# Attention and feed-forward on one core: plain fp32 for the first batch and for the value products, and a new order of the last matmuls

## The chip, the cores and the metric

The kernel runs on one core of a Trainium2 chip. The metric is the device time of one execution in microseconds, the median of three runs. Engines: TensorE (PE), VectorE (DVE), ScalarE (ACT), GpSimd (POOL) and the queues that issue transfers, above all SP.

## The reference

For 8 batches of 8 heads, 576 tokens and 64 channels a head, the reference computes two attentions in a row. A pack of 32 queries p attends over the keys and values; then the tokens q attend over the packed result, which is both key and value. The result, laid out as 576 x 512, goes through a Fourier mixing and a feed-forward:

```python
p_packed = sm_attn(p, k, v)
x = sm_attn(q, p_packed, p_packed)           # then (B, S, 512)
mixed = real(fft(fft(x, axis=1), axis=2))
u = x + mixed
un = (u - mean(u)) / sqrt(var(u) + 1e-6)
out = u + maximum(un @ w_ch1, 0) @ w_ch2     # 512 -> 2048 -> 512
```

The inputs q, k and p are drawn with a spread of 0.8.

## The kernel before

**Precision.** Most matmuls are done as three: each operand is split into a high part (rounded to fp32r, which TensorE takes in one pass) and a low part (the rest), and the products high x high, high x low and low x high are summed in PSUM (`three`, L279). `split` (L106) makes the parts: ScalarE rounds, VectorE or GpSimd subtracts. Some small products are plain fp32.

**Attention of one batch** is `front(b)` (L284), in two groups g of four heads. Scores are exponentiated, turned, and multiplied with the values (`packed`, L415); the packed result pp is spread into a block-diagonal matrix bd (128 rows of 4 heads x 32, 256 columns) by GpSimd, and split into bdh and bdl (`diagonals`, L437). In the second attention the weights a are normalised (`weights`), folded over the token mirror into even and odd sums (`folded`, L547, tiles eo and f; `folded_rest`, L560, makes the remaining columns of f and the rounded xh, oh; `folded_parts`, L598, the low parts xl, ol, fl). The Fourier transform over channels acts on pp (`values_spectrum`, L505: turned products and a join, parts gh and gl). Products of f with the spectrum give y (`first_products`, L687, for batch 0; the loop at L741 for the others), `spectrum` (L627) transforms over tokens into pz, and `value` (L672) multiplies the folded weights with bd into px, six matmuls for 512 columns of output. `even` (L772) adds px and one spectrum to pe, `blocks` (L777) makes the rows of u and their sums. 32 remaining token pairs go the same way through `spectra_apart` (L637) and L812 to L820.

**Feed-forward** (`ffn`, L888) takes tiles of four blocks of 128 rows, nine tiles in all. For each of 16 chunks, `up` is 12 matmuls into ph, ScalarE and VectorE make hh and hl, and `down` adds 12 matmuls into four accumulators, one step behind. At the end (L973 to L976) VectorE adds each accumulator to u and SP sends it out. Weights are fetched in chunks by SP during the head and tile 0 and rebuilt by ScalarE (`top`, `lows`) and VectorE (`bits`).

**Order.** Within a manual schedule each engine works in program order. For batch 0 that order is the string `ORDER[0]` (L40): each letter calls a function with its digit, as `n0` for `diagonals` of group 0, `F` `folded_high`, `h` `folded_parts`, `J` and `H` the low parts of g and f, `j` the join, `P` `first_products`, `X` the first value products, `T` the tables, `i` idle matmuls (`i122`: 12, waiting for tile m). The other batches are spread over the feed-forward steps of the tile before; `y` marks a step. Idle matmuls (L727) write a bank that nobody reads.

The last feed-forward group, whole:

```python
down(NJ - 1, *prev, nxt.moves(late[1]) if nxt and len(late) > 1 else ())
for i in (2, 3, 0, 1):
    u = u_of[keys[i]]
    nc.vector.scalar_tensor_tensor(u, acc[i], stat_of[keys[i]][:, 2:3], u, ALU.mult, ALU.add)
    nc.sync.dma_start(out[(first + i) * P:(first + i + 1) * P, :], u)
```

Of the kernel before, what the change touches and what calls it, by code (L numbers as in the profile page):

```python
# [17 lines left out]
P = 128  # L18
# [21 lines left out]
ORDER = ("K0 K1 V0 I0 Q0 W0 V1 Q1 B0 W1 W2 W3 i70 s0 x0 s1 i40 t0 x1 w0 p0 b0 T0 t1 n0 d0 v0 z0 i20 W4 W5 W6 W7 W8 W9 q0 e0 p1 "  # L40
         "b1 T1 T2 i80 l0 d1 w1 w2 w3 w4 m0 q1 a0 e1 g0 i122 l1 f0 r0 w5 F0 m1 n1 g1 w6 w7 i203 a1 j0 w8 h0 J0 H0 P0 f1 r1 F1 i64 j1 h1 J1 X0 "
         "H1 v2 W10 P1",
# [24 lines left out]
FR, FA, FO = 256, 357, 421  # L67
# [16 lines left out]
def tile_kernel(ctx, tc, kpT, qT, v, w1, w2, tabH, tabL, tabR, tabF, tabB, tabT, sel, ident_d, out):  # L84
# [32 lines left out]
    nc.gpsimd.memset(bmask, 0.0)  # L117
    for h in range(4):
        nc.gpsimd.memset(bmask[h * NPK:(h + 1) * NPK, h:h + 1], 0.5)
    w1f = cpool.tile([P, NJ, DM], F32, name="w1f")  # L120
# [14 lines left out]

    def load_tables(i):
        todo = [(basis, tabB)] + [x for t in range(2) for x in ((tbh[t], tabH[t]), (tbl[t], tabL[t]), (tbr[t], tabR[t]))] + [(tbf, tabF)]
        for to, src in (todo[:1], todo[1:3], todo[3:])[i]:
            nc.gpsimd.dma_start(to, src)
# [144 lines left out]
    def front(b):  # L284
        kps, vts, qts, e1s, e1T, rinv, away = {}, {}, {}, {}, {}, {}, {}
        pp2s, ppT, pph, ppl, bdh, bdl = {}, {}, {}, {}, {}, {}
        s2s, zs, as_, fh, fl, xh, xl, oh, ol, gh, gl = {}, {}, {}, {}, {}, {}, {}, {}, {}, {}, {}
# [127 lines left out]
        def packed(g):  # L415
# [16 lines left out]
            def spread():  # L432
                bd = work.tile([P, 4, D], F32, tag="tmp", name="bd", bufs=3)
                nc.gpsimd.tensor_tensor(bd, pp2[:, 0:1, :].to_broadcast([P, 4, D]),
                                        bmask.unsqueeze(2).to_broadcast([P, 4, D]), ALU.mult)

                def diagonals():  # L437
                    bdh[g] = work.tile([P, 4 * D], F32R, tag="bdh", name="bdh")
                    bdl[g] = work.tile([P, 4 * D], F32R, tag="bdl", name="bdl")
                    split(bdh[g], bdl[g], bd.rearrange("p a d -> p (a d)"), nc.gpsimd)  # L440

                if b == 0:
                    late["n", g] = diagonals
                else:
                    after(1, diagonals)
# [59 lines left out]
        def values_spectrum(g):  # L505

            hi = work.tile([P, 2, N2], F32R, tag="gh", name="gh")
            lo = work.tile([P, 2, N2], F32R, tag="gl", name="gl")
# [16 lines left out]
            def join():  # L525
                for t in range(2):
                    TW[TA[min(b, 2)]].tensor_tensor(prod[0][:, t, :], prod[0][:, t, :], prod[1][:, t, :], ops[t])
                if b == 0:
                    nc.scalar.copy(hi, prod[0])
                    late["J", g] = lambda: nc.vector.tensor_tensor(lo, prod[0], hi.bitcast(F32), ALU.subtract)  # L530
                else:
                    after(1, lambda: split(hi, lo, prod[0], TW[TL[min(b, 2)]]))
# [14 lines left out]
        def folded(g):  # L547
# [3 lines left out]
            f = work.tile([P, FW], F32, tag="att", name="f", bufs=ATT)  # L551
# [6 lines left out]
            eos[g], fs[g] = eo, f  # L558

        def folded_rest(g):  # L560
# [14 lines left out]
            def edge(at, op):  # L575
# [11 lines left out]
            sm.tensor_scalar(f[:, FA:FA + 64].rearrange("p (i m k) -> p i m k", i=2, m=2), apart, 2.0, 1.0 / 16,  # L587
                             ALU.mult, ALU.add)
            xh[g] = work.tile([P, 256], F32R, tag="xh", name="xh")
            nc.scalar.activation(xh[g], ec[:, 0:256], AF.Copy, bias=1.0 / 16)  # L590
            oh[g] = work.tile([P, 256], F32R, tag="oh", name="oh")
            nc.scalar.copy(oh[g], oc[:, 0:256])

        def folded_high(g):
            fh[g] = work.tile([P, FW], F32R, tag="fh", name="fh")
            nc.scalar.copy(fh[g], fs[g])

        def folded_parts(g):  # L598

            eo, f = eos[g], fs[g]  # L600
            ec, oc = eo[:, 0, :], eo[:, 1, :]
            if g not in fh:
                folded_high(g)
            xl[g] = work.tile([P, 256], F32R, tag="xl", name="xl")
            nc.vector.scalar_tensor_tensor(xl[g], ec[:, 0:256], 1.0 / 16, xh[g].bitcast(F32), ALU.add, ALU.subtract)
            ol[g] = work.tile([P, 256], F32R, tag="ol", name="ol")
            (nc.vector, nc.gpsimd)[EO[min(b, 2)]].tensor_tensor(ol[g], oc[:, 0:256], oh[g].bitcast(F32), ALU.subtract)

            def low():
                fl[g] = work.tile([P, FW], F32R, tag="fl", name="fl")  # L610
                nc.vector.tensor_tensor(fl[g], f, fh[g].bitcast(F32), ALU.subtract)

            in_place("H", g, low)
# [8 lines left out]
                 "F": folded_high, "z": lambda _: next(splits)}  # L622
        for x in "xblnjJH":
            parts[x] = lambda g, x=x: late[x, g]()
        yh, yl, yr, ysum, ypx, spec = [], [], [], [], {}, {}

        def spectrum(t, q, tag=None):  # L627

            pz = bank("pz")
            w = slice(P * q, P * q + P)  # L630
            three(pz[:, :N2], tbh[t][:, w], tbl[t][:, w], yh[t][:, q, :], yl[t][:, q, :], True, False)
            nc.tensor.matmul(pz[:, :N2], tbr[t][:NRC[t], w], yr[t][:NRC[t]], start=False, stop=True)
            sb = (ffp if tag else work).tile([P, N2], F32, tag=tag or f"spec{t}", name=f"spec{t}", bufs=6 if tag else 1)
            nc.scalar.copy(sb, pz[:, :N2])
            return sb

        def spectra_apart(rows):  # L637
# [22 lines left out]
            else:  # L660
                remainders(True, False)
                strips([[yh[t].bitcast(F32), yl[t].bitcast(F32)] for t in range(2)], False, True)
# [9 lines left out]
        def value(ah, al, w, px=None):  # L672
            px = bank("px") if px is None else px
            for g in range(2):
                three(px[:, g * 256:(g + 1) * 256], ah[g][:, w], al[g][:, w], bdh[g], bdl[g], True, True)
            return px

        def window(sb, rows):
            w = sb[rows, 0:256]
            return bass.AP(tensor=w.tensor, offset=w.offset, ap=[list(w.ap[0]), [1, 2], [1, 256]])  # L680
# [3 lines left out]
        def halves(x):  # L684
            return x.rearrange("p (a c) -> p a c", a=2)

        def first_products(g):  # L687
# [4 lines left out]
            for t in range(2 * g):  # L692
                yh.append(work.tile([P, 2, N2], F32R, tag="att", name="yh", bufs=ATT))
                yl.append(work.tile([P, 2, N2], F32R, tag="att", name="yl", bufs=ATT))
# [5 lines left out]
            for t, c in outs:  # L700
                nr, w, py = place(t, c)
                nc.tensor.matmul(py[:nr, :N2], fh[g][:, w], gh[g][:, t, :], start=(g == 0), stop=False)
                nc.tensor.matmul(py[:nr, :N2], fh[g][:, w], gl[g][:, t, :], start=False, stop=False)
                if g == 0:
                    nc.tensor.matmul(py[:nr, :N2], fl[g][:, w], gh[g][:, t, :], start=False, stop=False)
            for t, c in outs if g else ():
                nr, w, py = place(t, c)
                nc.tensor.matmul(py[:nr, :N2], fl[g][:, w], gh[g][:, t, :], start=False, stop=True)
            for t, c in outs if g else ():
                nr, w, py = place(t, c)  # L710
                if c < 2:
                    split(yh[t][:, c, :], yl[t][:, c, :], py[:, :N2])
# [8 lines left out]
        def first_values():  # L721
            ypx["p", 0] = value(xh, xl, slice(1, 256, 2))
            ypx["q", 0] = value(oh, ol, slice(1, 256, 2), psf.tile([P, 512], F32, tag="ph", name="px"))
# [17 lines left out]
        for t, base in enumerate((0, FO) if b else ()):  # L741
# [23 lines left out]
            whole = work.tile([P, 2, N2], F32, tag=("ysum", "gh")[t], name="ysum", bufs=1 + t)  # L765
            for c in range(2):
                nc.scalar.copy(whole[:, c, :], pys[c][:, :N2])
            ysum.append(whole)
# [3 lines left out]
        def even(c, A, px):  # L772
            pe = work.tile([P, DM], F32, tag="tmp", name="pe", bufs=3)
            nc.vector.tensor_tensor(halves(pe), halves(px), window(A, allp), ALU.add)
            return pe

        def blocks(c, pe, Bs, px):  # L777
            qe = work.tile([P, DM], F32, tag="tmp", name="qe", bufs=3)
            nc.vector.tensor_tensor(qe[:, 0:256], px[:, 0:256], Bs[:, 0:256], ALU.subtract)
            nc.vector.tensor_tensor(qe[:, 256:512], px[:, 256:512], Bs[:, 1:257], ALU.add)  # L780
# [7 lines left out]
        def odd_values(c):  # L788
            return value(oh, ol, slice(1 - c, 256, 2))

        if b == 0:
            for t in range(2):
                spec[t, 1] = spectrum(t, 1, "wr")
            ypx["p", 1] = value(xh, xl, slice(0, 256, 2))
            ypx["q", 1] = odd_values(1)
# [16 lines left out]
        px = value(fh, fl, slice(FA - rows.start, FA - rows.start + P))  # L812
        xa = work.tile([P, DM], F32, tag="tmp", name="xa", bufs=3)
        nc.vector.tensor_tensor(halves(xa[rows]), halves(px[rows]), window(A, rows), ALU.add)
        ur = u_of[kr]
        nc.vector.tensor_tensor(ur[rows, 0:256], xa[rows, 0:256], Bs[rows, 0:256], ALU.subtract)
# [349 lines left out]
```

## Time and profile before

| | us |
|---|---|
| median of 3 runs (965.23 to 966.66) | 965.59 |
| profiled execution | 964.36 |
| its span | 962.2 |
| TensorE busy in the span | 944.4 |
| VectorE, ScalarE, GpSimd busy | 589.5, 452.3, 463.2 |

The span is the time between the first and the last instruction that the profiler saw on the core; the time of the execution has 2.16 us around it. A view by stretch gives the busy time of each engine and the clock granted to TensorE as a share of full speed. The chain of waits goes back from the last instruction to what released each step. A group of instructions by form has its count, its busy time and the mean of one in nanoseconds.

### The profile page before, as it was taken

How to read it: one execution, taken by the hardware profiler on the slowest of the kernel's cores; microseconds unless marked ns; L12 is line 12 of the kernel's file. 1: busy time of each engine (PE TensorE's matmuls, PEld its weight loads, DVE VectorE, ACT ScalarE, POOL GpSimd, SP SyncE). 2: the span in 40 equal slices, each digit the busy share in tenths (PEclk: the TensorE clock that was granted, in tenths of full speed). 3: DMA queues.
4: the chain of work that ended last, by engine and by line, in shares of the span. 5: the costliest groups of instructions: out<-in, count | busy, mean ns of one | idle time of the engine just before them, and what ended most of it. 6: DMA issues, size and time to landing. Idle time of an engine off the chain costs nothing.

```text
span 962.2 us, 15191 instructions
## 1 busy us (share of the span) xinstructions
PE 944.4 (98%) x5614; PEld 774.4 (80%) x5614; DVE 589.5 (61%) x1186; ACT 452.3 (47%) x930; POOL 463.2 (48%) x397
## 2 busy tenths in 40 slices
PE   7899999999999999999999999999999999999997
PEld 4777887788778887788778877888778888887886
DVE  5989967684667756794668466874679353123112
ACT  5689564444434444444444444454444443233331
POOL 3156534653555435643465355543555355445442
PEclk9999999999999999999999999999999999999999
DMA  9675125400340016200540045100600011001001
GB/s 358 220 268 190 42 84 164 136 1 1 128 152 37 1 44 209 85 1 25 165 148 0 1 140 166 55 1 23 212 30 23 16 50 44 22 23 45 1 0 44
DMA packets 48777, 80.74 MB, mean 84 GB/s; under 512 B 7088, under 2 KB 28464, under 8 KB 48704
## 3 DMA queue, kind: packets, MB, share of 16 engines
q1 hardware_dynamic: 42480, 69.62, 21.3%
q10 hardware_dynamic: 5184, 8.85, 2.9%
q0 software_dynamic: 1040, 1.31, 0.5%
q8 instruction: 44, 0.72, 0.3%
q14 instruction: 29, 0.24, 0.1%
HBM read 59.45 MB, written 20.32 MB: 83 GB/s over the span
## 4 chain that ended last, share of the span: by engine, by line
PE 93%; DVE 3%; ACT 2%; DMA 1%; issue 1%; ACTq 0%; DVEq 0%
PE acc L927 40%; PE ph L910 40%; PE po L424 1%; PE px L282 1%; PE px L280 1%; PE px L281 1%; PE s2T L329 1%; PE py L282 1%; PE py L280 1%; PE py L281 1%; PE s L329 1%; ACT e L356 1%; PE idle L730 1%; PE pz L653 0%; DMA kp<-kpT 0%
## 5 line engine op out<-in xcount | busy, mean ns | idle before, releaser
L110 POOL TENSOR_TENSOR wr_l<-w2f,wr_h 128x512 fp32r<-128x512 f32 x144 | 188.2, 1307 | 275.8 <-ACT wr_h L107 269.8
L110 POOL TENSOR_TENSOR wr_l<-w1f,wr_h 128x512 fp32r<-128x512 f32 x144 | 200.3, 1392 | 195.2 <-ACT wr_h L107 175.6
L917 DVE SCALAR_TENSOR_TENSOR hl<-ph,hh 128x512 fp32r<-128x512 f32 x144 | 98.7, 686 | 288.3 <-ACT hh L916 287.6
L910 PE MATMUL ph<-uh,wr_h 128*128 128x512 f32 (+1 forms) x580 | 226.1, 392 | 1.0 <-ACT uh L107 1.0
L927 PE MATMUL acc<-wr_h,hh 128*128 128x512 f32 x576 | 226.0, 392 | 0.0
L927 PE MATMUL acc<-wr_h,hl 128*128 128x512 f32 x576 | 224.8, 390 | 0.0
L927 PE MATMUL acc<-wr_l,hh 128*128 128x512 f32 x576 | 224.8, 390 | 0.0
L910 PE MATMUL ph<-ul,wr_h 128*128 128x512 f32 (+1 forms) x580 | 224.2, 388 | 0.5 <-DVE ul L110 0.5
L910 PE MATMUL ph<-uh,wr_l 128*128 128x512 f32 (+1 forms) x580 | 224.1, 388 | 0.0
L916 ACT ACTIVATE hh<-ph 128x512 fp32r<-128x512 f32 x144 | 86.2, 598 | 235.6 <-PE ph L910 221.7
L107 ACT CAST wr_h<-w1f 128x512 fp32r<-128x512 f32 x144 | 89.3, 620 | 185.2 <-POOL wr_l L110 79.3
L910 PEld LDWEIGHTS ph<-uh,wr_h 128*128 128x128 f32 x580 | 108.5, 188 | 29.3 <-DVE s L479 5.9
L927 PEld LDWEIGHTS acc<-wr_h,hl 128*128 128x128 f32 x576 | 108.1, 188 | 23.2
L910 PEld LDWEIGHTS ph<-uh,wr_l 128*128 128x128 f32 x580 | 108.5, 188 | 22.7
L910 PEld LDWEIGHTS ph<-ul,wr_h 128*128 128x128 f32 x580 | 108.6, 188 | 21.6 <-DVE ul L110 0.9
L927 PEld LDWEIGHTS acc<-wr_h,hh 128*128 128x128 f32 x576 | 108.2, 188 | 21.7
L927 PEld LDWEIGHTS acc<-wr_l,hh 128*128 128x128 f32 x576 | 108.2, 188 | 20.9
L107 ACT CAST wr_h<-w2f 128x512 fp32r<-128x512 f32 x144 | 88.3, 613 | 34.1 <-PE acc L927 26.8
L975 DVE SCALAR_TENSOR_TENSOR ubuf<-acc,stat,ubuf 128x512 f32<-128x512 f32 x36 | 24.6, 744 | 3.5 <-PE acc L927 3.5
L834 DVE TENSOR_SCALAR unp<-ubuf,stat 128x512 f32<-128x512 f32 x28 | 25.4, 907 | 1.0 <-POOL bdl L110 0.7
L254 ACT ACTIVATE junk<-ubuf,stat 128x512 f32<-128x512 f32 x36 | 25.8, 717 | 0.2 <-DVE stat L249 0.2
L110 DVE TENSOR_TENSOR yl<-py,yh 128x258 fp32r<-128x258 f32 x32 | 13.2, 425 | 18.5 <-ACT yh L107 17.8
(230 smaller groups left out, 1216.7 us busy)
## 6 DMA issues: line engine op xcount, KB each, us to landing
kp<-kpT SPq DMA_DIRECT2D x16, 608.0 KB, 4.3
out<-ubuf SPq DMA_DIRECT2D x36, 256.0 KB, 3.9
far<-unt SPq DMA_DIRECT2D x28, 256.0 KB, 2.0
back<-far SPq DMA_DIRECT2D x112, 64.0 KB, 2.0
qt<-qT ACTq DMA_DIRECT2D x12, 576.0 KB, 4.6
vt<-v SPq DMA_DIRECT2D x12, 512.0 KB, 3.8
w1f<-w SPq DMA_DIRECT2D x9, 512.0 KB, 6.6
w2f<-w SPq DMA_DIRECT2D x9, 512.0 KB, 6.4
```

The source lines that it names most:

```text
L107: copied = nc.scalar.copy(hi, src)
L110: (lo_eng or nc.vector).tensor_tensor(lo, src, hi.bitcast(F32), ALU.subtract)
L254: nc.scalar.activation(junk, u, AF.Square, bias=st[:, 1:2], scale=-sign, accum_out=st[:, 2:3])
L280: nc.tensor.matmul(o, lh, rh, start=first, stop=False)
L281: nc.tensor.matmul(o, lh, rl, start=False, stop=False)
L282: nc.tensor.matmul(o, ll, rh, start=False, stop=last)
L834: nc.vector.tensor_scalar(un, u_of[key].rearrange("p (c q d) -> p q c d", c=4, q=4), stat_of[key][:, 1:2], None, ALU.subtract)
L910: nc.tensor.matmul(ph[:, t], l[:, c * P:(c + 1) * P], r[:, c, t], start=(k == 0), stop=(k == 11))
L916: nc.scalar.activation(hh[:, :T], ph[:, :T], AF.Relu)
L917: nc.vector.scalar_tensor_tensor(hl[:, :T], ph[:, :T], 0.0, hh[:, :T].bitcast(F32), ALU.max, ALU.subtract)
L927: nc.tensor.matmul(acc[i], l[:, w], r, start=(j == 0 and k == 0), stop=(j == NJ - 1 and k == 2))
L975: nc.vector.scalar_tensor_tensor(u, acc[i], stat_of[keys[i]][:, 2:3], u, ALU.mult, ALU.add)
```

## The change

Batch 0 works in plain fp32 from the fold on: f, the joined spectrum and y have no high and low parts, the tables of `spectrum` are loaded whole (tabS), and the order of its steps is new. Its value products are fp32 with the 256-column bd. From batch 1 on the value products are plain fp32 too, with a bd of two heads (128 columns): the upper 64 rows (two heads) and the lower 64 rows are separate matmuls on their own half of the array, into a PSUM bank each. The last feed-forward group of the last tile is done in another order, its last block in two halves of columns. The core of the diff:

```diff
-... p0 b0 T0 t1 n0 d0 v0 z0 i20 W4 W5 W6 W7 W8 W9 q0 e0 p1 b1 T1 T2 i80 l0 d1 w1 w2 w3 w4 m0 q1 a0 e1 g0 i122 l1
-   f0 r0 w5 F0 m1 n1 g1 w6 w7 i203 a1 j0 w8 h0 J0 H0 P0 f1 r1 F1 i64 j1 h1 J1 X0 H1 v2 W10 P1
+... p0 b0 T0 t1 d0 v0 z0 i20 W4 W5 W6 W7 W8 W9 q0 e0 p1 b1 T1 i80 l0 d1 w1 w2 w3 w4 m0 q1 a0 e1 g0 i122 l1
+   f0 j0 r0 w5 m1 g1 P0 w6 w7 a1 f1 r1 j1 X0 w8 v2 W10 P1 T2
 def load_tables(i):
+    if i == 1:
+        whole.append(spot(0, 7, [P, 2, KT]))
+        todo = [(whole[0], tabS...)] + [(tbr[t], tabR[t]) for t in range(2)] + [(tbf, tabF)]
+    else:
+        todo = [(basis, tabB)] if i == 0 else [x for t in range(2) for x in ((tbh[t], tabH[t]), (tbl[t], tabL[t]))]
 def spread():
-    bd = work.tile([P, 4, D], F32, ...)
...
-    bdh[g], bdl[g] = ...; split(bdh[g], bdl[g], bd, nc.gpsimd)
+    mask, n = (bpair, 2) if b else (bmask, 4)
+    bd[g] = work.tile([P, n, D], F32, tag=f"bd{n}", name="bd")
 def join():
-    if b == 0:
-        nc.scalar.copy(hi, prod[0])
-        late["J", g] = lambda: nc.vector.tensor_tensor(lo, prod[0], hi, ALU.subtract)
+    # batch 0: the join writes gh itself, fp32
 def folded_rest(g):
-    f[:, FA:FA + 64] = ...
-    xh[g] = F32R; oh[g] = F32R
+    fa[g] = work.tile([P, D], F32, ...)
+    xs[g] = F32;  os_[g] = F32
 def folded_parts(g):
-    xl[g] = ...; ol[g] = ...
     fh[g], fl[g] = ...                       # batch 1 on only
 def spectrum(t, q, tag=None):
+    if b: three(...)
+    else: nc.tensor.matmul(pz[:, :N2], whole[0][:, t, w], yh[t][:, q, :], start=True, stop=False)
-def value(ah, al, w, px=None):
-    for g in range(2):
-        three(px[:, g * 256:(g + 1) * 256], ah[g][:, w], al[g][:, w], bdh[g], bdl[g], True, True)
+def values_of(*pairs, rows=slice(0, P), banks=(None, None)):
+    if b == 0:
+        # one fp32 matmul of 256 columns for each pair and g
...
+    banks = [bank("px") for _ in range(2)]
+    for k, (x, w) in enumerate(pairs):
+        for g in range(2):
+            for r in range(2):
+                at = slice(r * D, (r + 1) * D)
+                nc.tensor.matmul(banks[r][rows, k * 256 + g * P:k * 256 + (g + 1) * P], x[g][at, w], bd[g][at],
+                                 start=True, stop=True, tile_position=(r * D, rows.start))
+def add_even(to, px, A, rows):
+    for x, cols in pieces(px):
+        nc.vector.tensor_tensor(halves(to[rows])[:, :, cols], x[rows], window(A, rows, cols), ALU.add)
+def add_odd(to, px, Bs, rows):
+    for x, cols in pieces(px):
+        for g, op in enumerate((ALU.subtract, ALU.add)):
+            nc.vector.tensor_tensor(halves(to[rows])[:, g, cols], x[rows, g, :], Bs[rows, cols.start + g:cols.stop + g], op)
 def first_products(g):
-    # high x high, high x low (and low x high) for each of six outputs; yh, yl split
+    nc.tensor.matmul(py[:nr, :N2], fh[g][:, w], gh[g][:, t, :], start=(g == 0), stop=(g == 1))
...
+    nc.scalar.copy(yh[t][:, c, :], py[:, :N2])
 c-th full step (batch 1 on):
-    pe = even(c, A, value(xh, xl, slice(1 - c, 256, 2)))
-    blocks(c, pe, Bs, odd_values(c))
+    px, qx = values_of((xs, slice(1 - c, 256, 2)), (os_, slice(1 - c, 256, 2)))
+    blocks(c, even(c, A, px), Bs, qx)
 remaining rows:
-    px = value(fh, fl, slice(FA - rows.start, FA - rows.start + P))
+    px, = values_of((fa, slice(0, D)), rows=rows)
 ffn, last tile, last chunk:
+    down(j - 1, *prev, pair=pairs[0], to=(0, 1, 2))
+    for k, i in ((1, 0), (0, 3), (1, 1), (1, 2), (1, 3)):
+        down(j - 1 + k, *(prev, cur)[k], pair=pairs[k], to=(i,))      # the last one by halves of columns
-for i in (2, 3, 0, 1):
+for i in (2, 3, 0, 1) if nxt is not None else range(4):
+    # last tile, i == 3: two halves of columns, the second sent out on ScalarE's queue
```

## Rows read from the trace of the kernel before

**Rows 1.** The page, part 1: busy time, share of the span, instructions.

```profile
PE 944.4 (98%) x5614; PEld 774.4 (80%) x5614; DVE 589.5 (61%) x1186; ACT 452.3 (47%) x930; POOL 463.2 (48%) x397
```

**Rows 2.** Stretches: length, engines' busy us (instructions), clock, transfer share, GB/s.

```profile
0.00:50.00 50.00, 40.24 (x378) 31.36 (x378) 38.21 (x100) 30.59 (x64) 12.97 (x32) 0.97 0.75 278
...
100.00:900.00 800.00, 797.77 (x4611) 657.04 (x4611) 497.11 (x994) 362.64 (x753) 394.42 (x321) 1.00 0.21 68
...
940.00:962.20 22.20, 16.73 (x74) 13.51 (x72) 4.82 (x7) 4.05 (x7) 5.21 (x4) 0.98 0.13 47
```

**Rows 3.** Chain of waits, the head: start us, length us, engine, tile, line.

```profile
22.55 4.46 PE idle L730 x24
...
28.79 1.17 DVE s L539
...
30.76 0.65 DVE turned L527 x2
...
32.79 0.89 DVE fl L611
...
40.35 0.39 ACT yh L107
...
41.24 0.39 PE pz L280
...
43.20 0.56 DVE pe L774
...
48.77 0.61 DVE ul L110
```

**Rows 4.** Chain of waits, the middle: tiles 1 and 2.

```profile
164.02 0.12 PE px L280
...
164.72 2.74 PE acc L927 x12
...
180.78 0.27 PE s2Tt L329 x16
181.05 0.86 PE s2T L329 x16
181.91 2.95 PE ph L910 x12
...
188.07 2.72 PE ph L910 x12
...
239.67 0.12 PE px L280
...
241.12 2.74 PE acc L927 x12
```

**Rows 5.** Chain of waits, the tail: first and last of VectorE's four outputs.

```profile
956.16 0.62 DVE ubuf L975
...
958.25 0.66 DVE ubuf L975
```

**Rows 6.** Instructions in order of time, head: start us, us, engine, line, operation.

```profile
20.34 0.72 DVE L539 TENSOR_TENSOR s<-s,z 128x576 f32<-128x576 f32 x1
...
27.10 0.24 POOL L587 TENSOR_SCALAR f<-a 128x64 f32<-128x64 f32 x1
...
27.62 4.54 PE L730 MATMUL idle<-ubuf,z 128*18 128x128 f32 x40
...
28.60 0.73 POOL L110 TENSOR_TENSOR bdl<-bd,bdh 128x256 fp32r<-128x256 f32 x1
...
36.27 0.76 DVE L527 TENSOR_TENSOR turned<-turned 128x258 f32<-128x258 f32 x2
```

**Rows 7.** Groups by form, weight loads: busy us, mean ns of one.

```profile
L864 PEld LDWEIGHTS untp<-ident,un 128*128 128x128 f32 x32 | 3.9, 140 | 2.0 <-ACT un L994 1.8
...
L730 PEld LDWEIGHTS idle<-ubuf,z 128*18 128x18 f32 x40 | 3.8, 98 | 0.6
```

**Rows 8.** Stretches of 2 us in the head, columns as in rows 2.

```profile
24.00:26.00 2.00, 2.00 (x11) 1.44 (x10) 1.93 (x5) 1.97 (x6) 0.37 (x1) 0.50 1.11 395
```

More of the change, by code (lines that the diff above doesn't have):

```diff
@@ L83, in tile_kernel @@
 @with_exitstack
-def tile_kernel(ctx, tc, kpT, qT, v, w1, w2, tabH, tabL, tabR, tabF, tabB, tabT, sel, ident_d, out):
+def tile_kernel(ctx, tc, kpT, qT, v, w1, w2, tabS, tabH, tabL, tabR, tabF, tabB, tabT, sel, ident_d, out):
     nc = tc.nc
@@ L432, in spread @@
             def spread():
[L433 to L440, printed above, removed]
-                if b == 0:
-                    late["n", g] = diagonals
-                else:
-                    after(1, diagonals)
+                mask, n = (bpair, 2) if b else (bmask, 4)
+                bd[g] = work.tile([P, n, D], F32, tag=f"bd{n}", name="bd")
+                nc.gpsimd.tensor_tensor(bd[g], pp2[:, 0:1, :].to_broadcast([P, n, D]), mask.unsqueeze(2).to_broadcast([P, n, D]),
+                                        ALU.mult)
             in_place("b", g, spread)
@@ L505, in values_spectrum @@
         def values_spectrum(g):
-            hi = work.tile([P, 2, N2], F32R, tag="gh", name="gh")
-            lo = work.tile([P, 2, N2], F32R, tag="gl", name="gl")
+            hi = work.tile([P, 2, N2], F32R if b else F32, tag="gh", name="gh")
+            lo = work.tile([P, 2, N2], F32R, tag="gl", name="gl") if b else None
             TW = (nc.gpsimd, nc.vector)
@@ L586, in folded_rest, with folded_parts @@
             apart = bass.AP(tensor=a.tensor, offset=a.offset + 256, ap=[list(a.ap[0]), [1, 2], [NE, 2], [2, 16]])
[L587 to L594, printed above, removed]
-            fh[g] = work.tile([P, FW], F32R, tag="fh", name="fh")
[L596 to L613, printed above, removed]
+            fa[g] = work.tile([P, D], F32, tag="fa", name="fa")
+            sm.tensor_scalar(fa[g].rearrange("p (i m k) -> p i m k", i=2, m=2), apart, 2.0, 1.0 / 16, ALU.mult, ALU.add)
+            xs[g] = work.tile([P, 256], F32, tag="xh", name="xs")
+            nc.scalar.activation(xs[g], ec[:, 0:256], AF.Copy, bias=1.0 / 16)
+            os_[g] = work.tile([P, 256], F32, tag="oh", name="os")
+            nc.scalar.copy(os_[g], oc[:, 0:256])
+        def folded_parts(g):
+            f = fs[g]
+            fh[g] = work.tile([P, FW], F32R, tag="fh", name="fh")
+            nc.scalar.copy(fh[g], f)
+            fl[g] = work.tile([P, FW], F32R, tag="fl", name="fl")
+            nc.vector.tensor_tensor(fl[g], f, fh[g].bitcast(F32), ALU.subtract)
         parts = {"S": lambda _: scores(0, 1), "U": lambda _: queries(0, 1), "D": lambda _: scores_away(0, 1),
@@ L630, in spectrum @@
             w = slice(P * q, P * q + P)
-            three(pz[:, :N2], tbh[t][:, w], tbl[t][:, w], yh[t][:, q, :], yl[t][:, q, :], True, False)
+            if b:
+                three(pz[:, :N2], tbh[t][:, w], tbl[t][:, w], yh[t][:, q, :], yl[t][:, q, :], True, False)
+            else:
+                nc.tensor.matmul(pz[:, :N2], whole[0][:, t, w], yh[t][:, q, :], start=True, stop=False)
             nc.tensor.matmul(pz[:, :N2], tbr[t][:NRC[t], w], yr[t][:NRC[t]], start=False, stop=True)
@@ L773, in even @@
             pe = work.tile([P, DM], F32, tag="tmp", name="pe", bufs=3)
-            nc.vector.tensor_tensor(halves(pe), halves(px), window(A, allp), ALU.add)
+            add_even(pe, px, A, allp)
             return pe
@@ L918, in up, with down @@
             return hh, hl
-        def down(j, hh, hl, moves=()):
+        def down(j, hh, hl, moves=(), pair=None, to=range(n)):
             moves = list(moves)
-            vh, vl = ready.pop(0)
-            for i in range(n):
+            vh, vl = pair or ready.pop(0)
+            for i in to:
                 w = slice(i * P, (i + 1) * P)
-                for k, (l, r) in enumerate(((hh, vh), (hh, vl), (hl, vh))):
-                    nc.tensor.matmul(acc[i], l[:, w], r, start=(j == 0 and k == 0), stop=(j == NJ - 1 and k == 2))
-                    if moves:
-                        moves.pop(0)()
+                halved = nxt is None and j == NJ - 1 and i == n - 1
+                for cols in (slice(0, DM // 2), slice(DM // 2, DM)) if halved else (slice(0, DM),):
+                    for k, (l, r) in enumerate(((hh, vh), (hh, vl), (hl, vh))):
+                        nc.tensor.matmul(acc[i][:, cols], l[:, w], r[:, cols], start=(j == 0 and k == 0),
+                                         stop=(j == NJ - 1 and k == 2 and cols.stop == DM))
+                        if moves:
+                            moves.pop(0)()
         def less(*ks):
@@ L959, in ffn @@
             sends(2 * j)
+            if nxt is None and j == NJ - 1:
+                pairs = [ready.pop(0), None]
+                down(j - 1, *prev, pair=pairs[0], to=(0, 1, 2))
+                pairs[1] = ready.pop(0)
+                for k, i in ((1, 0), (0, 3), (1, 1), (1, 2), (1, 3)):
+                    down(j - 1 + k, *(prev, cur)[k], pair=pairs[k], to=(i,))
+                break
             if prev is not None:
@@ L968, in ffn @@
             prev = cur
-        down(NJ - 1, *prev, nxt.moves(late[1]) if nxt and len(late) > 1 else ())
-        if nxt and len(late) > 1:
-            nxt.parts(late[1])
-        next(splits, None)
-        for i in (2, 3, 0, 1):
+        if nxt is not None:
+            down(NJ - 1, *prev, nxt.moves(late[1]) if len(late) > 1 else ())
+            if len(late) > 1:
+                nxt.parts(late[1])
+            next(splits, None)
+        for i in (2, 3, 0, 1) if nxt is not None else range(4):
             u = u_of[keys[i]]
-            nc.vector.scalar_tensor_tensor(u, acc[i], stat_of[keys[i]][:, 2:3], u, ALU.mult, ALU.add)
-            nc.sync.dma_start(out[(first + i) * P:(first + i + 1) * P, :], u)
+            for cols in (slice(0, DM // 2), slice(DM // 2, DM)) if nxt is None and i == 3 else (slice(0, DM),):
+                nc.vector.scalar_tensor_tensor(u[:, cols], acc[i][:, cols], stat_of[keys[i]][:, 2:3], u[:, cols],
+                                               ALU.mult, ALU.add)
+                (nc.sync if cols.start == 0 else nc.scalar).dma_start(out[(first + i) * P:(first + i + 1) * P, cols], u[:, cols])
             free.append(place_of[keys[i]])
@@ L1126, in _prepare @@
     }
-    for n, t in zip(("tabH", "tabL", "tabR", "tabF", "tabB", "tabT", "sel", "ident_d"), _tables()):
+    for n, t in zip(("tabS", "tabH", "tabL", "tabR", "tabF", "tabB", "tabT", "sel", "ident_d"), _tables()):
         arrays[n] = t
```

102 lines of the change are left out of this document (54 added, 48 removed).

## The prediction

> **What bounds the kernel now.** I read the page first: TensorE is busy for 98% of the span [rows 1], so an edit counts only if it shortens TensorE's own queue, or a stretch in which that queue waits. The table of stretches says where these are: 9.8 of the first 50 us are free, 2 of the 800 from 100 to 900, 5.5 of the last 22 [rows 2]. The chain of waits then gives three stages, each with its own limit.
>
> Head (0 to 52 us): a chain over VectorE, ScalarE, GpSimd and TensorE. The reader sees on it a block of idle matmuls, an s multiplication of 1.17 us, a join, the low parts up to fl, and pe, the start of the first blocks, at 43.20 [rows 3]. Middle: TensorE has no gap; a feed-forward step of 12 matmuls is 2.72 us, and what TensorE does for attention stands between two steps and adds its full length [rows 4]. Tail: after the last matmul VectorE still walks over outputs until 958.91 [rows 5].
>
> The profiled execution took 964.36 us, 2.16 more than its span of 962.2 and 1.23 below the median of the runs, 965.59. I sum against 964.36 and add 1.23 at the end.
>
> **1. The head, batch 0.** All high and low parts go here. The price of a plain fp32 matmul first. It is recorded as two instructions: 40 of them with 128 moving columns take 4.54 us, 0.113 each [rows 6], by which 258 columns cost 2 x 0.113 x 258/128 = 0.46; s2T, two passes of 512 columns, takes 0.86 [rows 4], by which they cost 0.43. I take 0.44, against 3 x 0.12 for the split form (px, [rows 4]).
>
> Now along the chain.
>
> - Until 27.3 nothing moves. The idle block that waits for m holds TensorE from 22.55 to 27.01 [rows 3]. The join of the first half (0.65 by the other half's) now stands ahead of the second half's sums on VectorE, but the subtraction after these waits on GpSimd anyway, whose small folds end at 27.34 [rows 6]. I allow 0.1 for a slip; without that cover it would be 0.65.
> - n1 goes. Its subtraction on GpSimd (0.73 at 28.60) ran beside the s multiplication of 1.17; the same operation with GpSimd quiet took 0.72 [rows 3, 6]. So -0.5.
> - Between the transposed weights (30.76) and the fold of the second half stood the join, xl, ol, gl and fl, until 33.68 [rows 3]. All leave this place; the fold begins at about 30.4. Together -3.2.
> - Fold, rest and second join, which ended at 37.03 [rows 6], end at 33.8.
> - After the join came the cast of gh, gl, fl and the last low products; the first copy of a product began at 40.35, the spectrum at 41.24 [rows 3]. Now the six products of the second half follow the join: 6 x 0.44, 33.8 to 36.45, copied by ScalarE as each is done. The spectrum starts at 36.45: -4.8.
> - yl is gone between copy and spectrum, and a spectrum is 0.44 + 0.12 instead of 4 x 0.12. With 0.2 for the end of the matmul and 0.4 for the copy, pe starts at 37.6 instead of 43.20.
> - From pe to ul (5.6 us [rows 3]) the chain stays, with 0.15 for qe, whose spectrum is copied after one more y.
>
> Head: 37.6 + 0.15 - 43.20 = **-5.4 us**. The first half's products (27.6 to 30.3) and the first values (until 32.9) lie in what were idle matmuls; about 1 us of waiting for the join is left behind them as their cover. Transfers: the feed-forward asks for weights relative to its own steps, so they move with it; tabS goes out on GpSimd's queue in tabH's place, behind fewer transfers than before and some 19 us ahead of its use; the late tables stand behind everything on that queue and are read a tile later. W10 and v2 keep their neighbours on SP and VectorE. Ends: -3.2 (only what lies before the second join) to -7 (if the shorter ScalarE queue gains too).
>
> The remaining rows of batch 0: 8 records of strips less, four at a time, 2 x 0.22, so -0.45; the values grow from 6 x 0.12 to four instructions of 0.22 (+0.2). **-0.2**.
>
> **2. Value products from the second batch on.** Seven batches, in each two full steps and one of remaining rows. Before, a full step is 12 matmuls, 239.67 to 241.12, and the feed-forward step behind it takes 2.74: 1.47 over. Remaining rows: 164.02 to 164.72, and again 2.74: 0.72 over [rows 4].
>
> After, a full step is 8 matmuls of 64 rows and 128 moving columns, 16 records: 8 x 0.107 = 0.86 if the two halves run together. That halves can is in the s2T row: 16 records of 512 columns on tiles of 64 rows by 32 columns took 0.86, the time of two one behind the other, so eight ran at a time, both row halves among them [rows 4].
>
> What no plain sum has is the change of the array's shape. s2Tt and s2T take 0.27 + 0.86 where their columns need 0.11 + 0.86, and the feed-forward step after them takes 2.95, not 2.72 [rows 4]: 0.16 + 0.23 = 0.39. I take **0.4** for in and out together. Full step: 0.86 + 0.4 = 1.26 against 1.47, so -0.21, 14 times -2.9. Remaining rows: 4 x 0.107 + 0.4 = 0.83 against 0.72, so +0.11, seven times +0.8. **-2.1 us**.
>
> Bounds. Below, with the change of shape free: -0.61 x 14 - 0.29 x 7 = -10.6. Above, with the halves one after the other: full step 16 x 0.113 + 0.4 = 2.21 (+0.74 x 14), remaining rows 8 x 0.113 + 0.4 = 1.30 (+0.58 x 7), +14.4. I stand by the s2T row, which has the same 64-row halves, fp32 and the same neighbours; only 128 output columns instead of 32 are new.
>
> Do the loads keep up? A load of 18 columns is recorded with 98 ns, one of 128 with 140 [rows 7]: 0.38 ns a column, some 0.05 us for 128. Two of them fit into the 0.107 of a pair.
>
> The Trainium skill (TensorE: Matmul & The Clock Gate, Part 3, "What overlaps and what doesn't") speaks against this: a weight load overlaps with matmuls in flight only where its row group differs. By it, the second load of each half would wait for that half's first matmul. The trace does not agree: in a feed-forward step each matmul has its own 128-column load on all rows, and 12 of them take 2.72, 0.227 each, where 512 columns alone need 0.215 (s2T, [rows 4]); no room for a load is left outside. What the rule would give is the second rival.
>
> VectorE gets two operations for even and four for odd where it had one and two; even at 0.4 for each of the three more, 1.2 us, this fits into what it has free, 38% between 100 and 900 us [rows 2], and xl and ol and GpSimd's split of bd go in other steps. None of this is on the path, so I count nothing; if hl of the next feed-forward step came late for it, a step would lose up to those 1.2. The second bank of the remaining rows was last read by the scores' second exp, shortly before; without that cover some tenths a batch.
>
> **3. The tail.** Before, VectorE starts its first output at 956.16 and ends its fourth at 958.91 [rows 5]; issue and transfer make 3.3 more. After, two outputs are done before the last matmul, the third runs at 956.2 as the first does now (0.62), and the halves of the last (between 0.33 and 0.62 each; I take 0.4) follow, the second when its matmuls are done, 957.25 to 957.65. That is -1.25. The last transfer is half as large, on ScalarE's queue, idle then; -0.25. The new order wants the last hh and hl one block of three matmuls earlier, 2.0 instead of 2.7 us after their up step; ScalarE and VectorE have one operation each before that and nothing else. **-1.5 us** (ends -1 and -2).
>
> **Sum**: -5.4 - 0.2 - 2.1 - 1.5 = -9.2. Own time 955.2; against the median **956.4 us**.
>
> **Rivals.**
> - *The halves don't overlap (slower).* Place: the value steps. Price +14.4 in place of -2.1: 965.6 - 7.1 + 14.4 = 972.9. The whole turns slower once a full step costs above 1.9 us. For it: no row has two tiles of 64 rows with 128 output columns. Against it: s2T. 7%.
> - *Loads wait within a half.* A pair costs 0.107 + 0.05: full step 8 x 0.157 + 0.4 = 1.66 (+0.19 x 14), remaining rows, 64 columns, 4 x 0.132 + 0.4 = 0.93 (+0.21 x 7): +4.1, 962.6. Against it the feed-forward step. 8%. (It is the rule of the Trainium skill named above.)
> - *The change of shape is cheap*: -10.6, 947.9. For it: the price may come from the many small tiles of s2T. 8%.
> - *TensorE's clock falls in the head*, since idle blocks that kept it up are gone. After a stretch almost without matmuls the row from 24 to 26 us shows 0.50 of full speed [rows 8], 1.2 GHz. Between 33 and 40 us that would double some 5 us of products, spectra and values: 961.4. Against it: the new products fill 27.6 to 32.9, and the gap is 1 us. 9%.
> - *The head's gain is half eaten*, by ScalarE, where the w tops stand right before the xs copies, or by VectorE's order: 959.1. 8%.
>
> **Numbers.** The forecast itself has 60%, 954 to 959. From 950.5 to 963 lies some 85%: without the cheap change, the serial halves and a part of the loads. 0.2% is 1.9 us, about what a measurement tells from no change. Faster (below 963.7): forecast, cheap change, clock, half head, three quarters of the loads, 91%, less 5% for what I overlooked: 0.86. Same 0.06, slower 0.08 with the serial halves.
>
> **What would show it.** Head: pe near 37.6, the first feed-forward matmul 5.4 us earlier, granted clock 1.00 from 28 us on. Middle: px records in pairs, a full step of 1.2 to 1.3 us with its after-effect, remaining rows 0.1 longer than before. Tail: VectorE's last operation 0.9 us after the last matmul. Wrong, if px records stand 0.11 apart without overlap, if TensorE waits for VectorE behind a value step, or if pe comes after 40.

## The result and the profile after

The changed kernel takes **956.32 us** (median of 5 runs, 956.01 to 957.28) against 966.21 for the kernel before on the same chip (5 runs): ratio 0.9902, 95% interval [0.9889, 0.9916], 8 to 11 us less. The forecast was 956.4. The sum is right; one of its terms is right only because a miss was made up by something that the prediction didn't have, and that was luck.

Busy time, share of the span and instructions of each engine, after:

```profile
PE 939.8 (98%) x5601; PEld 759.1 (80%) x5601; DVE 571.1 (60%) x1196; ACT 444.8 (47%) x910; POOL 450.7 (47%) x387
```

TensorE is as full as it was [rows 1], with 4.6 us less to do. Two stretches (length, busy us and instructions of PE, PEld, DVE, ACT, POOL, then clock, transfer share, GB/s):

```profile
0.00:50.00 50.00, 40.20 (x364) 28.97 (x364) 35.12 (x94) 30.88 (x64) 15.26 (x38) 0.97 0.79 286
100.00:900.00 800.00, 799.25 (x4689) 649.05 (x4688) 482.17 (x1008) 357.50 (x738) 384.89 (x311) 1.00 0.21 68
```

The head is no denser than it was; it is shorter. In the middle 0.75 us are free where there were 2.23 [rows 2]: that is the first sign of a gain nobody had counted.

The chain of waits through the head, after (start, length, what):

```profile
22.55 0.71 DVE m L485
...
29.78 0.68 DVE s L536
...
33.87 0.43 DVE gh L527
34.30 0.04 issue
34.34 2.88 PE py L720 x12
37.23 0.43 PE pz L620 x2
...
38.23 0.04 DVE pe L698
...
43.93 0.61 DVE ul L110
...
46.77 1.70 PE ph L917 x12
```

Two lines of the same view before, which rows 3 lack:

```profile
21.79 0.72 DVE m L485
...
51.61 1.70 PE ph L910 x12
```

m starts 0.76 later than in the profile before. Its start differs between executions of one kernel: in e0_again below, the kernel before once more, it is 22.26, in the profiles of the three parts 21.83 to 22.09. So the head is read from m on: m to pe took 21.41 us and takes 15.68; m to the first feed-forward matmuls of the chain (ph, the second half of the first step) took 29.82 and takes 24.22. s is back at 0.68 [rows 3], and behind the last join (gh) the products stand on the chain alone.

The chain in the middle, after: one full value step and one of remaining rows, each with the step behind it, and an undisturbed step:

```profile
130.66 1.14 PE px L677 x16
131.81 2.94 PE acc L936 x12
...
142.58 2.72 PE ph L917 x12
...
159.31 0.58 PE px L677 x8
159.89 2.94 PE acc L936 x12
```

A full step costs 1.14 + 0.22 = 1.36 (before 1.47), remaining rows 0.80 (before 0.72) [rows 4].

The tail, after, in the chain:

```profile
944.84 4.09 PE acc L936 x18
...
949.03 0.62 DVE ubuf L994
...
949.70 0.66 DVE ubuf L994
...
950.41 0.48 DVE ubuf L994
```

and its last matmul and VectorE's last four operations in the view by time:

```profile
950.03 0.28 PE L936 MATMUL acc<-wr_h,hl 128*128 128x256 f32 x1
949.03 2.25 DVE L994 SCALAR_TENSOR_TENSOR ubuf<-acc,stat,ubuf 128x512 f32<-128x512 f32 x4 [0.61 <-PE acc L936]
```

VectorE ends at 951.28, 0.97 behind the last matmul (950.31). Before, the last matmul was

```profile
956.34 0.39 PE L927 MATMUL acc<-wr_h,hl 128*128 128x512 f32 x1
```

and VectorE ended 2.18 behind its end [rows 5].

### The profile page after: what moved, and what is told of

It reads as the page before. It is cut to its first block, busy times and chain, and to the rows that moved or that the text cites. A ratio compares the mean times of both kernels' runs of the same rounds, so it can differ in the third digit from the quotient of the medians.

```text
span 954.4 us, 15154 instructions
## 1 busy us (share of the span) xinstructions
PE 939.8 (98%) x5601; PEld 759.1 (80%) x5601; DVE 571.1 (60%) x1196; ACT 444.8 (47%) x910; POOL 450.7 (47%) x387
## 4 chain that ended last, share of the span: by engine, by line
PE 94%; DVE 3%; ACT 1%; DMA 1%; issue 1%; ACTq 0%; DVEq 0%
PE acc L936 41%; PE ph L917 41%; PE px L677 2%; PE po L433 1%; PE s2T L338 1%; PE s L338 1%; PE py L290 1%; PE py L291 1%; PE py L289 1%; ACT e L365 0%; DMA kp<-kpT 0%; PE pz L642 0%; PE pz L621 0%; PE pg L516 0%; PE pg L514 0%
## 5 line engine op out<-in xcount | busy, mean ns | idle before, releaser
L994 DVE SCALAR_TENSOR_TENSOR ubuf<-acc,stat,ubuf 128x512 f32<-128x512 f32 (+1 forms) x37 | 24.8, 728 | 2.1 <-PE acc L936 2.1
L267 POOL TENSOR_TENSOR stat<-stat,mhalf 128x1 f32<-128x1 f32 x36 | 25.5, 721 | 0.0
L599 DVE TENSOR_TENSOR fl<-f,fh 128x712 fp32r<-128x712 f32 x14 | 19.0, 1356 | 9.2 <-ACT fh L597 9.0
```

The costliest lines, as they stand in the source:

```text
L267: nc.gpsimd.tensor_tensor(st[:, 2:3], st[:, 2:3], mhalf, ALU.pow)
L994: nc.vector.scalar_tensor_tensor(u[:, cols], acc[i][:, cols], stat_of[keys[i]][:, 2:3], u[:, cols], ALU.mult, ALU.add)
```

## The experiments

**The three parts, each alone in the kernel before, and the kernel before once more.** The edits are those of the diff: all of batch 0 (e1_head), the value products from batch 1 on (e2_values), the last group (e3_tail).

> Only the edits of batch 0 (plain fp32 from the fold on, whole tables, the new order), with the split value products from batch 1 on and the old tail. Theory (the three stages add up): the head alone gives most, -5.5 to -7 us against the kernel before (ratio 0.9930 to 0.9943), first pe at about 38 us, and the middle keeps its px rows of 1.45 us and its 2 us of TensorE waits between 100 and 900 us. Rival (the head's gain is partly what the value products give through a shorter ScalarE and GpSimd queue): under -4.5 us.

> Only the value products from batch 1 on (fp32, two 64-row halves), head and tail as before. Theory A (what the trace after shows counts as matmuls only): a full step 1.14 us and an after-effect of 0.22, so -0.09 a full step and +0.09 for the remaining rows, 14 and 7 times: -0.6 us, and the TensorE waits of the kernel before (2.2 us between 100 and 900 us) stay. Theory B (the lighter ScalarE, VectorE and GpSimd also take away waits): -1.5 to -2.5 us, and TensorE's free time between 100 and 900 us falls below 1 us. The prediction had -2.1 by the matmuls alone.

> Only the last feed-forward group in the new order, its last block in halves, the last half sent out on ScalarE's queue. Theory: -1.4 to -1.6 us, VectorE's last operation 1.9 to 2.0 us after the start of its output for block 2 instead of 2.75. Rival (the transfer that ends last does not start earlier, or takes longer because two queues share it): 0 to -0.7 us.

> The kernel before once more, for a second profile. Theory: the first 22 us vary from execution to execution (in the profile before, the second m started at 21.79 us, in the profile after at 22.55, with the same operations ahead of it), so its time lies between 964.4 and 966.7, and what differs from the first profile lies before 22 us. Rival: the difference comes from the changed kernel's own order; then the second m is at 21.8 again.

| | us | ratio | share |
|---|---|---|---|
| before, same chip (17 runs) | 965.54 | | |
| e1_head | 960.03 | 0.9940 [0.9927, 0.9952] | -5.8 |
| e2_values | 963.28 | 0.9970 [0.9959, 0.9981] | -2.9 |
| e3_tail | 964.13 | 0.9987 [0.9978, 0.9996] | -1.25 |
| e0_again (one run) | 967.56 | | |

The shares add up to -9.95, about the whole gain. Each has an interval of about 1 us to either side, so this shows no more than that no large term is missing. e0_again misses its expectation (966.7 at most, all of the difference ahead of 22 us): its m is 0.47 later than in the first profile of before, out of 3.2 us; its waits for po, below, are 2.5 more. And e2_values gives 1.8 to 4.0 us, where its rows give 14 x 0.11 - 7 x 0.08 = 1.0, although its head was slower in the profile (m to the first ph of the chain 31.46, clock 0.92 from 0 to 50 us). That is theory B: TensorE's free time from 100 to 890 us is 0.63 in it, 2.23 before. What TensorE waits for before the packed products (po), between 50 us and the end, in the profile of before, in e2_values (no po row at all) and after (line waited for: us in all, times, longest):

```profile
PE po L424 <- ACT hh L916: 0.8, 1, 0.8
PE po L424 <- ACT junk L254: 0.5, 1, 0.5
PE po L424 <- DMA e1T<-fare: 0.3, 1, 0.3
```

```profile
PE ph L956 <- ACT uh L107: 0.9, 2, 0.7
PE ph L956 <- DVE ul L110: 0.5, 1, 0.5
```

```profile
PE po L433 <- DMA e1T<-fare: 0.2, 1, 0.2
```

In e0_again it is 4.1 us. po reads weights that go out to memory and back (fare, e1T). Where ScalarE is named, it is the way back all the same that comes late: transfers of e1T land at 585.79 and 690.04, and po begins at 585.88 and 690.24.

**What a value step costs.** Two edits to the changed kernel, in `values_of`:

```diff
 e5_order: halves one after the other
-for k, (x, w) in enumerate(pairs):
-    for g in range(2):
-        for r in range(2):
+for r in range(2):
+    for k, (x, w) in enumerate(pairs):
+        for g in range(2):
 e6_double: every value matmul twice
-for k, (x, w) in enumerate(pairs):
+for k, (x, w) in enumerate(pairs * 2):
+    k %= len(pairs)
```

> The changed kernel with the loop over the row halves r outermost in values_of: the eight (or four) matmuls of rows 0 to 63 are issued first, then those of rows 64 to 127; same matmuls, same results. Theory (in the changed kernel two matmuls of different row halves stream together, which is why a full step costs 1.36 us and not 2.2): issued one half after the other they can't, so the row of a full step grows from 1.14 to about 2.0 us (+0.86, 14 times) and that of the remaining rows from 0.58 to about 1.0 (+0.43, 7 times): about +15 us, 971. Rival (they never overlapped; a record pair is bounded by something else): the rows stay within 0.1 and the time within 2 us of 956.3.

> The changed kernel with each value matmul from the second batch on, and in the first, issued twice (same result). It separates what the columns cost from what the change of the array's shape costs. Theory (pairs stream at 0.107 us, and 0.4 to 0.5 us are paid once per step for the change of shape): the full-step row grows by 0.86, from 1.14 to 2.0 us, and that of the remaining rows by 0.43, from 0.58 to 1.0; what is left after subtraction, 1.36 - 0.86 = 0.5 with the after-effect, is the change of shape. Rival (weight loads wait inside a half: a pair costs 0.16): +1.25 and +0.53. Whole kernel +15 us by the theory, +21 by the rival, less what the rows hide in waits.

e5_order 964.24 (10 runs), 7.9 above the changed kernel; e6_double 972.78 (one run). The chain in e5_order, then in e6_double:

```profile
130.60 1.72 PE px L677 x16
...
160.39 0.59 PE px L677 x8
```

```profile
130.70 2.08 PE px L678 x32
132.79 2.94 PE acc L937 x12
...
161.23 1.02 PE px L678 x16
162.25 2.99 PE acc L937 x12
```

Doubling adds 0.94 to a full step and 0.44 to remaining rows. So the columns cost 0.94 and what is left, 0.20 ahead and 0.22 behind, is the change of the array's shape: 0.42 (remaining rows 0.14 and 0.22). The halves do run together: out of pairs a full step needs 0.58 more (14 x 0.58 = 8.1, the 7.9 measured). But the expected 0.86 isn't reached, and the remaining rows lose nothing. TensorE's records in e5_order show why:

```profile
130.53 0.74 PE L677 MATMUL px<-bd,xs 64*128 64x128 f32 x4
131.10 0.28 PE L677 MATMUL px<-bd,os 64*128 64x128 f32 x1
131.11 0.38 PE L677 MATMUL px<-bd,xs 64*128 64x128 f32 x1
...
131.69 0.63 PE L677 MATMUL px<-bd,os 64*128 64x128 f32 x4
```

By these records the first half's two xs matmuls (four records) run alone; then its os matmuls run beside the second half's xs, which stand behind them in the program. That makes three groups of four slots (0.57, 0.59, 0.56) instead of two, so order matters less than I expected.

**The clock and the chain in the head.** The changed kernel without its idle block `i122` (e7_noidle), and with four more VectorE additions behind the second fold (e9_chain):

```diff
 e7_noidle
-... a0 e1 g0 i122 l1 f0 j0 ...
+... a0 e1 g0 l1 f0 j0 ...
 e9_chain: folded(), after the fourth fold operation
+if b == 0 and g == 1:
+    for i in range(4):
+        nc.vector.tensor_tensor(more[:, 0:256], ec[:, 0:256], oc[:, 0:256], ALU.add)
```

> The changed kernel without the block of idle matmuls i122 in the first batch (the 4.5 us ahead of the join). Theory of the prediction's clock rival: without them TensorE's granted clock falls below 1.00 between 28 and 40 us and products, spectra and first values there run at up to twice their time: pe 2 to 5 us later, whole kernel +2 to +5. Rival (the products and values of the first half keep the clock up by themselves): pe within 0.5 us of 38.2 and the whole within 0.7 us of 956.3.

> The changed kernel with four more VectorE additions (128 x 256, results not used) in the first batch, right after the fold of the second half, some 1.35 us of VectorE time. Theory (VectorE's own chain from m through s, fold, rest and join sets pe, so each us that the change takes from it comes off the whole): pe 1.35 us later and the whole +1.35 us, 957.7. Rival (TensorE or ScalarE's copies set pe, and VectorE has slack there): pe and the whole within 0.4 us.

e7_noidle 956.39, ratio 0.9907 [0.9891, 0.9924] to before, the same as the changed kernel; m to pe takes 15.67. The idle block of the changed kernel gained no time. Without it the clock does stay low for longer, and the first half's products take 4.70 instead of 2.77, but they have room; it is back at 1.00 ahead of the second half's (columns as above):

```profile
26.00:28.00 2.00, 1.62 (x3) 0.90 (x4) 1.90 (x6) 2.00 (x6) 1.72 (x8) 0.50 1.06 404
28.00:30.00 2.00, 2.00 (x6) 1.45 (x6) 2.00 (x4) 1.76 (x4) 2.00 (x3) 0.58 1.02 407
30.00:32.00 2.00, 1.59 (x8) 1.08 (x7) 1.90 (x5) 0.59 (x2) 1.34 (x3) 1.00 1.04 418
```

e9_chain 959.07, ratio 0.9929 [0.9914, 0.9944]: +2.75, twice what the chain theory gave. Its join ends 1.72 later, which is that theory: the four additions take 1.71 on the chain, not 1.35. (Counted from m it is 2.1; 0.4 of that lies ahead of the additions.) The rest is the prediction's clock rival; stretches, then the chain:

```profile
34.00:36.00 2.00, 0.00 (x0) 0.00 (x0) 1.93 (x12) 0.00 (x0) 0.00 (x0) 1.00 1.15 388
36.00:38.00 2.00, 1.94 (x6) 1.50 (x7) 0.94 (x3) 0.63 (x2) 0.00 (x0) 0.64 0.69 191
38.00:40.00 2.00, 2.00 (x6) 1.52 (x5) 0.61 (x2) 0.87 (x3) 0.00 (x0) 0.51 0.84 270
```

```profile
36.06 4.57 PE py L724 x12
```

TensorE has nothing to do for two us ahead of the last join, its clock goes to 1.2 GHz, and the products take 4.57 instead of 2.88. A join 1.7 us later than the changed kernel's was enough for that.

**Why the waits for po went.** In before, the second of two fetches (fare from e1b) takes 0.62 and 0.86 us to issue in the last two of six tiles (the expectation of e10_shift has 0.73 for the first, which is e0_again's), 0.33 elsewhere. Is it the place in SP's stream (e10_shift: three small loads more on SP ahead of it), and is the interval to po in truth set by the way through memory (e11_fill: the remaining rows' products done twice)?

```diff
 e10_shift
+for i in range(1, 4):
+    nc.sync.dma_start(selT[:, 8 * i:8 * i + 8], ident_d[:, 0:8])
 e11_fill
 px = value(fh, fl, slice(FA - rows.start, FA - rows.start + P))
+if b:
+    value(fh, fl, slice(FA - rows.start, FA - rows.start + P), px)
```

> The kernel before with three more small loads (128 x 8 columns of the identity, not used) on SP's queue early on, so that all of SP's later instructions come three places later in its stream. In the profile of before two of the fetches of turned weights (fare from e1b) take 0.73 to 0.86 us to issue where the others take 0.33, and land later. Theory (this hangs on the place in SP's stream, which the change shifts): the slow issues go or move to another tile, TensorE's waits for the packed products between 100 and 890 us shrink from 1.6 us to under 0.8, and the whole is 0.5 to 1.5 us shorter. Rival (it hangs on something else, such as GpSimd's traffic): the slow issues stay at 0.7 to 0.9 in the same two tiles and the whole is within 0.5 us of before.

> The kernel before with the remaining rows' value product issued twice from the second batch on: +0.70 us of TensorE, seven times, 4.9 us in all, between the scores and the packed products that read the weights back from memory. Theory (in that interval TensorE waits for the round trip of the weights in part of the tiles, so what is added there is partly free): +1.1 to +3.3 us, and TensorE's idle time between 100 and 890 us falls from 2.2 us to under 1. Rival (TensorE's queue alone counts there): +4.9 us, and the waits stay.

e10_shift 964.68 against 965.15, ratio 0.9994 [0.9983, 1.0004]: no difference shown, and the same two tiles are slow (0.68 and 1.02); not SP's place. e11_fill 967.70, ratio 1.0027 [1.0017, 1.0037]: 4.9 us more of TensorE work cost 1.6 to 3.6. That is what the theory of a partly free interval gave, but e11_fill doesn't settle it: it changes TensorE's stream alone, and in it no issue is slow any more, which takes waits away as well (TensorE's idle time from 100 to 890 us is 1.15; under 1 was expected). That led to the view of the transfer queues: in before a 16 KB transfer on the instruction queue lies in the very moment of each slow issue, and of none of the ten others. There are 44 of them, one for 2 x 5614 / 44 = 255 of TensorE's recorded matmuls and loads, so I take them for TensorE's code. I moved them: more or fewer idle matmuls in the head of the kernel before.

```diff
 e12_code
-... g0 i122 l1 ...
+... g0 i42 N18 l1 ...        # N18: 18 idle matmuls of 8 columns
 e13_later
-... g0 i122 l1 ...
+... g0 i72 l1 ...
```

> The kernel before with the idle block of the first batch's 12 matmuls of 128 columns as 4 of 128 and 18 of 8 columns: ten matmuls (some 40 recorded instructions of TensorE) more, in about the same time, so that all of TensorE's later code stands 40 instructions further back. In the profile of before a transfer of code (16 KB on the instruction queue, 44 in the run, one for every 255 matmuls and loads) lies 4.5 us after the start of the scores in exactly the two tiles whose fetch of turned weights is slow to issue, and 2.0 to 3.0 us after it in the four others. Theory (the code transfer and the slow issue belong together): code is now fetched 4.5 us earlier, before the fetch of turned weights in every tile; all issues take 0.33, TensorE's waits for the packed products fall below 0.8 us, and the whole is 0.8 to 1.8 us shorter than before. Rival (coincidence): two slow issues in the last two tiles as before, time within 0.5 us.

> The kernel before with 7 instead of 12 idle matmuls in that block: some 20 recorded instructions of TensorE fewer, so that its code is fetched 2.3 us later in each tile. Theory (as for the run with more idle matmuls): the code transfer now meets the fetch of turned weights (4.3 to 5.7 us after the scores' start) in the first four tiles, whose issues become slow (0.7 to 1.0 us), and leaves the last two, whose issues become 0.33; the whole 0 to 1.5 us longer than before. Rival (coincidence): the slow issues stay in the last two tiles; the time within 0.5 us.

e13_later 969.20, ratio 1.0031 [1.0020, 1.0042]: five idle matmuls fewer, 2 to 4 us slower, more than the 0 to 1.5 expected. SP's two issues in a tile together, before (a tile that is not slow and the last, which is), the first tile of e13_later, and a tile of e12_code:

```profile
475.35 1.29 SPq L375 DMA_DIRECT2D fare<-e1b  x2
...
682.82 1.82 SPq L375 DMA_DIRECT2D fare<-e1b  x2
```

```profile
163.64 1.66 SPq L375 DMA_DIRECT2D fare<-e1b  x2
```

```profile
582.26 1.29 SPq L375 DMA_DIRECT2D fare<-e1b  x2
```

In e13_later the first five tiles are slow, the first four of them newly so; the last two were to be freed and aren't. The code transfer of all six begins 4.6 to 4.8 us behind the scores. In the sixth the issue takes 0.32 and the fetches land late all the same (3.3 and 3.0 us after issue instead of 2.1), and po waits 1.2 there: it is the landing that counts. The queue's row (packets, MB, share) in its first tile, and what TensorE waited for in that kernel:

```profile
q8 instruction: 1, 0.02, 3.5%
```

```profile
PE po L424 <- DMA e1T<-fare: 4.4, 4, 1.6
PE po L424 <- ACT hh L916: 2.0, 2, 1.2
```

That is shown, then: TensorE's code and SP's fetch collide, and it costs up to 1.6 us a tile. e12_code, the opposite shift, has its code 1.2 to 3.0 us behind the scores and no slow issue in any tile, as the theory said (though the code moved by less than 4.5 us). Its time, 965.43, ratio 0.9992 [0.9983, 1.0001], is not shown to differ, and so misses the 0.8 to 1.8 us less that were expected: po still waited 1.8 us, between its two halves, and the clock in its head fell (0.83 from 28 to 40 us), the first ph of the chain coming at 53.70 instead of 51.61. So the collision accounts for the waits ahead of po, 1.3 of 1.6 us in before.

The change took the collision away without aiming at it: it has another number of TensorE instructions, and so have e1_head and e2_values, each of which alone has no slow issue in any tile. The second half of po is another matter. It waits for the last transfer back, which lands 11.6 to 12.7 us behind the scores where po waits in e0_again and e12_code, and 11.1 to 11.6 after the change. e1_head, without a collision, still waits 1.6 us for po, most of it there. Why these waits are gone after the change stays open.

## Why the prediction was right, step by step

- **Head, -5.4**: right. From m to the first ph of the chain it is -5.60; e1_head alone gives -5.8 with the interval of its ratio from -4.6 to -7.0, in which the end of the collision is contained. Taken from m, with the start of m in before, the join ends at 33.54 (forecast 33.8), the spectrum begins at 36.47 (36.45), pe at 37.47 (37.6). VectorE's chain sets the join and the products behind it set pe, as e9_chain shows.
- **The clock rival**: it didn't come true, but it isn't far: e9_chain is what it looks like. The row from 28 to 40 us has 1.00 after. What kept it there for the products of the second half was work and not the idle block, by e7_noidle.
- **Remaining rows of batch 0, -0.2**: +0.15. The strips (pz of these rows) gave their 0.44; the four fp32 products cost 1.01 instead of 0.70; and the two steps around them take 0.28 more. I put that down to their 64 output columns, a change of shape too, which I had not counted; no run shows it apart.
- **A term that nobody counted**: in the batches behind, the products pg of the channel transform cost 0.50 instead of 0.47 and the step behind them 0.03 more, twice a batch, some 0.8 us over seven batches. e1_head has it and e2_values hasn't, so it belongs to the edits of the head; its cause is open.
- **Value products, -2.1**: the sum is right (e2_values: -2.9, -1.8 to -4.0), the term is not. The rows gave -1.0 in place of -2.1. The step that failed is "8 x 0.107 = 0.86 if the two halves run together": four pairs of matmuls take 0.94 by e6_double, 0.02 more a pair, so a full step is 1.36 and not 1.26, -0.11 and not -0.21. The price of the change of shape, taken as 0.4 from s2T, measured 0.42. What made it good was TensorE's waiting for po, 1.6 us in the profile of before and 0.2 after. That is luck: 1.3 of it hung on where code transfers fell, and the prediction has no term for it. It saw 2 us free in the middle and let them stand; the rows of waits would have said what they were.
- **Halves one after the other, loads that wait**: both refuted. Serial halves cost +0.58 a step where made so (e5_order). Pairs that wait for loads would have added 8 x 0.157 = 1.25 when doubled; it was 0.94. The rule of the Trainium skill named in the prediction (TensorE: Matmul & The Clock Gate, Part 3, "What overlaps and what doesn't") doesn't hold for these loads at the price that I gave it. That price was itself misread: 0.38 ns a column compares an 18-column load with one of another kind, while px loads of 64 and 128 columns are recorded after with 132 and 192 ns. So 128 columns are nearer 0.1 us than 0.05, and a pair that waited would have cost more still. Nor does the row of s2T give 0.215 for 512 columns of a feed-forward matmul; the tail after does, where matmuls of 256 columns come 0.12 apart and those of 512 columns 0.227, 0.22 for 512 columns alone.
- **Tail, -1.5**: -1.2 for VectorE's end, as forecast within 0.05, and -0.2 for the transfer; e3_tail alone -1.25 with -0.4 to -2.1, where -1.4 to -1.6 was expected.
- **Own time and median**: the profiled execution of before was 964.36 and its kernel's medians 965.2 to 966.2; the pair of profiles differs by 8.04, where the terms had -9.2, and the medians by 9.9. Of the difference between the two, 0.76 is the later m; the rest may be waits for po, of which the profile of before has fewer than e0_again. That 956.32 fell on 956.4 to a tenth is luck as well.

## What to carry to other kernels

A run of matmuls in another tile shape cost a fixed price at its two ends, here 0.42 us together for a full step and 0.36 for the remaining rows; count such runs before columns. Idle time of a full engine has a name: look up what it waits for even where it is 0.3% of the span. And after any change of an instruction count, look whether a code transfer now meets a transfer that somebody waits for: it can give or take more than the edit itself.

## What the runs showed of the hardware

- In 14 of the 84 tiles in the 14 profiles here (those of before, e0_again, e3_tail, e10_shift, e13_later) a 16 KB transfer of TensorE's code begins 0.2 to 0.5 us behind the first of SP's two fetches. In all of them the first fetch lands 2.7 to 3.3 us after its issue, instead of 2.0 to 2.2 in all but one of the 70 others (2.6 in e6_double, with a code transfer 2.1 us behind that fetch), and in 13 the second takes 0.52 to 1.02 us to issue, instead of 0.33. Five idle matmuls fewer, 130 us and more ahead, moved the transfer onto four more tiles and cost 3.0 us.
- By the records, matmuls on the two halves of the array don't keep the program's order: in e5_order the second half's xs start at 131.11, ahead of the first half's last os, and remaining rows issued half by half cost no more than in pairs (0.59 and 0.58).
- After two us without matmuls the granted clock was 0.64 and 0.51 in the next two stretches of two us (e9_chain), 1.2 GHz for most of them, with TensorE busy all the while.
